# A weight tile's low part is subtracted after the next tile's VectorE steps, and ScalarE adds 1e-9 to the softmax sums

## The chip, the cores and the metric

The kernel runs on one core of a Trainium2 chip (trn2). The metric is the device time of one execution in microseconds (us); lower is better. The engines are TensorE (PE; PEld is its loading of weights), VectorE (DVE), ScalarE (ACT), GpSimd (POOL) and SyncE (SP, which here issues the DMAs).

## The reference

Causal attention by blocks of 64 positions feeds two dense blocks of the kind "linear, nonlinearity, linear". All inputs and outputs are float32.

```python
# q, k, v: (4, 8, 576, 64)
scores = np.where(mask, scale * q @ k.T, -1e9)      # mask: block_i >= block_j
scores = scores - scores.max(-1, keepdims=True)
attn = np.exp(scores)
attn = attn / (attn.sum(-1, keepdims=True) + 1e-09)
x = (attn @ v)                                       # as 2304 tokens x 512
h = np.maximum(x @ w_in, 0.0);  x = (h * h) @ w_out  # w_in 512x2048, w_out 2048x512
h = x @ w_in2                                        # second block, same sizes
g = (a0 + a1*h + a2*h**2 + a3*h**3) / (1 + |b0|*|h| + |b1|*h**2 + 1e-6)
out = g @ w_out2
```

The weights arrive as 64-bit floats (8 bytes for each element, read as pairs of 32-bit words).

## The kernel before

**Products.** A product that must be accurate is made of three reduced-precision products. Each operand is kept as a high part (a rounded copy) and a low part (the original minus that copy), and `PAIRS = ((0, 0), (1, 0), (0, 1))` sums high times high, weight-low times data-high, and weight-high times data-low (L482, L495, L707, L747, L816). The first ten of the 32 heads ("plain", the "float32 heads" of the change) are computed in plain float32 instead, without parts.

**Stages.** A list of slots runs through the attention: in each slot one or two 128-row tiles of one head get their scores (PE, L294), their row maxima (DVE, L315), their exponentials with row sums (ACT, L328), their transposes (PE L370, copied out of PSUM by ACT, L388 and L400) and, some slots later, the product with v (PE, L429 or L442). Between these, the matmuls of the first half of the first dense block (`ha`, `ya`, L482 and L495) are dealt out step by step. After the attention come the second half of that block (`hb`, `yb`, L707 and L747) and then the second dense block (`hc`, `yc`, L707 and L816).

**Normalizing a plain head pair.** After the exponentials of an odd head, DVE adds 1e-9 to the sums of both heads (L340) and takes the reciprocal (L341), POOL spreads these over 64 columns each (`rb`, L344), PE transposes the spread tile (`rows`, L436), ACT copies it (L437), and DVE multiplies the product with v by it (L438, `xp`). POOL then makes the high and low parts of the result (`xt`, L451 and L452). POOL also scales the queries of later heads (`qr`, L228) ahead of the scores.

**Converting a weight tile.** `Converter.step` handles one tile of 128x512 weights per call. ACT makes the magnitude of the upper words (L117), DVE runs four instructions (L118 and L119 on the raw words, L121 and L122 on the result tile `cv`), and SP's queue brings the raw tile (L93). L122, "the bits", is the last: after it `cv` is a float32 tile, and the raw buffer (three of them) is free for a later tile. In the *next* call ACT copies `cv` to the high part (L110) and POOL subtracts to get the low part (L111). The tiles are named `ai` and `ao` (first half of block one, w_in and w_out), `bi` and `bo` (second half), `ci` and `co` (block two).

**Order.** The code is written slot by slot, but a scheduler that simulates the engines decides the order in which each engine's queue holds its instructions; each queue then runs in order. `issue_after` in the code ties an instruction to another for that scheduler.

Of the kernel before, what the change touches and what calls it, by code (L numbers as in the profile page):

```python
# [9 lines left out]
F32R = mybir.dt.float32r  # L10
U32 = mybir.dt.uint32
AF = mybir.ActivationFunctionType
ALU = mybir.AluOpType
# [4 lines left out]
P = 128  # L18
# [7 lines left out]
HALF = NM // 2  # L26
# [18 lines left out]
def f(ap):  # L45
    return ap.bitcast(F32)
# [3 lines left out]
def attention_moe_moe(ctx: ExitStack, tc: tile.TileContext, q, k, v, wi1, wo1, wi2, wo2, a, b, out):  # L50
    nc = tc.nc
# [17 lines left out]
    cab = const.tile([P, 8], F32, name="cab")  # L69
# [6 lines left out]
        name=nc.get_next_instruction_name(), act_func_set_id=EXP_LN_SET, ins=[], outs=[]))  # L76
# [4 lines left out]
    class Converter:  # L81
# [21 lines left out]
                self.step()  # L103

        def step(self):
            if self.mid:
                c, (nm, _, wp, kind, store, key, eng) = self.mid
                self.mid = None
                w = wp.tile([P, 2, 512], F32R, tag="w" + kind, name=f"w_{nm}", bufs=HALF)
                nc.scalar.activation(w[:, 0, :], c, AF.Copy)  # L110
                eng.tensor_tensor(w[:, 1, :], c, f(w[:, 0, :]), op=ALU.subtract)  # L111
                store[kind, key] = w
            if self.raws:
                raw, job = self.raws.pop(0)
                c = self.pool.tile([P, 512], F32, tag="cv", name=f"cv_{job[0]}", bufs=2)
                low, high, cu = raw[:, :, 0], raw[:, :, 1], c.bitcast(U32)
                nc.scalar.activation(c, high.bitcast(F32), AF.Abs, scale=65536.0)  # L117
                nc.vector.tensor_scalar(low, low, 2.0 ** -29, 7.0, op0=ALU.mult, op1=ALU.min)  # L118
                nc.vector.scalar_tensor_tensor(  # L119
                    low, high, 0x80000000, low, op0=ALU.bitwise_and, op1=ALU.bitwise_or)  # L120
                nc.vector.tensor_scalar(c, c, 2.0, 122880.0 * 65536.0, op0=ALU.max, op1=ALU.min)  # L121
                nc.vector.scalar_tensor_tensor(  # L122
                    cu, cu, 3, low, op0=ALU.logical_shift_left, op1=ALU.bitwise_or)
                if job[2] is None:

                    nc.sync.dma_start(job[4][job[5]], c)
                else:
                    self.mid = (c, job)
            self.load()

    PAIRS = ((0, 0), (1, 0), (0, 1))
# [10 lines left out]
    for pool in (attn, early):  # L142
        psets.append([])
        for t in range(5):
            w_ = P * (t + 1)
# [12 lines left out]
    def ptile(un, t):  # L158
        own = psets[un.hd % 2 if un.hd < H else 0]
        if un.gis == (0, 1) and un.hd % 4 > 1:  # L160
            return own[4][:, 0:3 * P] if t == 2 else own[3][:, P * t:P * (2 * t + 1)]
        return own[t]
# [94 lines left out]
    for st in sts:  # L257
        nc.vector.memset(st, 1.0)

    sums = [attn.tile([P, 2, 2, 8], F32, name=f"sums{n}") for n in range(2)]  # L260
    for sm in sums:
        nc.vector.memset(sm, 1.0)
# [70 lines left out]
    def emit_norm(i):  # L333
        st = stats.pop(i)
        un, gi = slots[i]
        if un.plain:
            if un.hd % 2 and gi % 2:
                sm = sums[un.hd // 2 % 2]
                t0, t1 = TILES[gi // 2]
                nc.vector.tensor_scalar(sm[:, 1, :, t0:t1], sm[:, 0, :, t0:t1], 1e-9, None, op0=ALU.add)  # L340
                nc.vector.reciprocal(sm[:, 1, :, t0:t1], sm[:, 1, :, t0:t1])  # L341
                rb = attn.tile([P, t1 - t0, P], F32, tag="rb", name=f"rb{un.hd}_{gi}", bufs=2, padded_shape=[P, 3, P])
                for t in range(t0, t1):
                    nc.gpsimd.tensor_scalar(  # L344
                        rb[:, t - t0].rearrange("p (n d) -> p n d", n=2),
                        sm[:, 1, :, t:t + 1].to_broadcast([P, 2, D]), 1.0, 0.0, op0=ALU.mult, op1=ALU.add)
                spread[un.hd, gi // 2] = rb
            return
        g = GROUPS[slots[i][1]]
        n = len(g)  # L350
        nc.vector.tensor_scalar(st[:, 4:4 + n], st[:, 2:2 + n], 1e-9, None, op0=ALU.add)
        nc.vector.reciprocal(st[:, 6:6 + n], st[:, 4:4 + n])  # L352
        for n, t in enumerate(g):
            r = D if t == 0 else 0
            pv = ptile(slots[i][0], t)[r:P, 0:P * t + D]
            nc.gpsimd.tensor_scalar(pv, pv, st[r:P, 6 + n:7 + n], 0.0, op0=ALU.mult, op1=ALU.add)  # L356
# [221 lines left out]
    for i in range(NI + 5):  # L578
# [7 lines left out]
        if 0 <= i - 1 < NI:  # L586
            emit_norm(i - 1)
# [88 lines left out]
    def tmp(tag, n, nm, dt=F32):  # L676
        return g2.tile([P, n], dt, tag=tag, name=nm, bufs={"t": 3, "o": 1}.get(tag, 2), padded_shape=[P, 512])
# [43 lines left out]
    for u in range(len(units) + LAG):  # L721
        if u < len(units):
            j, m = units[u]
            t0, n = blocks2[j]
# [9 lines left out]
        if u >= LAG:  # L734
            j, m = units[u - LAG]
            t0, n = blocks2[j]
# [33 lines left out]
    mid, gf = {}, {}  # L770
    for u in range(len(units) + LAG):
# [7 lines left out]
        if u - 1 in mid:  # L779
            r, w, t = mid.pop(u - 1)  # L780
# [7 lines left out]
        if u < len(units):  # L788
            j, m = units[u]
            t0, n = blocks3[j]  # L790
# [7 lines left out]
            ab, w, t = tmp("ab", n, f"ab{u}"), tmp("w", n, f"wq{u}"), tmp("t", n, f"t{u}")  # L798
# [7 lines left out]
        if u >= LAG:  # L806
            j, m = units[u - LAG]
            t0, n = blocks3[j]
# [76 lines left out]
```

## Time and profile before

| what | value |
|---|---|
| median of 3 runs | 1020.05 us (1020.04 to 1020.3) |
| the profiled execution's own time | 1022.03 us |
| its span, first to last instruction | 1020.2 us |
| PE busy in the span | 995.7 us (98%) |
| DVE, ACT, POOL busy | 727.6, 722.2, 582.6 us |

The span is the stretch that the trace covers; the remaining 1.8 us of the profiled execution lie around it. "Idle before" in a row is time in which the engine stood still ahead of that instruction, with the releaser that ended it. The ends of matmuls are modelled, so PE can read as busy while its matmuls are not at their densest.

### The profile page before, as it was taken

How to read it: one execution, taken by the hardware profiler on the slowest of the kernel's cores; microseconds unless marked ns; L12 is line 12 of the kernel's file. 1: busy time of each engine (PE TensorE's matmuls, PEld its weight loads, DVE VectorE, ACT ScalarE, POOL GpSimd, SP SyncE). 2: the span in 40 equal slices, each digit the busy share in tenths (PEclk: the TensorE clock that was granted, in tenths of full speed). 3: DMA queues.
4: the chain of work that ended last, by engine and by line, in shares of the span. 5: the costliest groups of instructions: out<-in, count | busy, mean ns of one | idle time of the engine just before them, and what ended most of it. 6: DMA issues, size and time to landing. Idle time of an engine off the chain costs nothing. (4 is left out here: it accounts for less than half of the span.)

```text
span 1020.2 us, 17058 instructions
## 1 busy us (share of the span) xinstructions
PE 995.7 (98%) x5721; PEld 884.1 (87%) x5721; DVE 727.6 (71%) x1412; ACT 722.2 (71%) x1620; POOL 582.6 (57%) x632
## 2 busy tenths in 40 slices
PE   7999999999999999999999999999999999999997
PEld 5677999999999999999788888887888888899996
DVE  6798587768767646786667666887766766777766
ACT  7779687768777746564455557787787776788775
POOL 5677686768676745630232448767466554655552
PEclk9999999999999999999999999999999999999999
DMA  9766334243432204457655572001101100100000
GB/s 302 221 201 210 120 99 150 92 117 111 118 93 81 67 31 149 167 193 247 234 174 187 171 249 95 1 1 41 42 1 32 42 1 1 50 24 1 32 1 31
DMA packets 63894, 106.58 MB, mean 104 GB/s; under 512 B 16064, under 2 KB 34496, under 8 KB 63808
## 3 DMA queue, kind: packets, MB, share of 16 engines
q1 hardware_dynamic: 63520, 105.34, 32.0%
q8 instruction: 45, 0.74, 0.3%
q14 instruction: 41, 0.34, 0.1%
q10 hardware_dynamic: 288, 0.16, 0.1%
HBM read 79.17 MB, written 23.07 MB: 100 GB/s over the span
## 5 line engine op out<-in xcount | busy, mean ns | idle before, releaser
L816 PE MATMUL yc<-w_co,gc 128*128 128x512 f32 x864 | 211.8, 391 | 3.1 <-ACT gc L776 3.1
L707 PE MATMUL hc<-xc,w_ci 128*128 128x512 f32 (+1 forms) x960 | 211.2, 368 | 0.0
L707 PEld LDWEIGHTS hc<-xc,w_ci 128*128 128x128 f32 x960 | 176.1, 188 | 26.3
L816 PEld LDWEIGHTS yc<-w_co,gc 128*128 128x128 f32 x864 | 161.1, 188 | 36.0 <-ACT gc L776 4.6
L777 POOL TENSOR_TENSOR gc<-t,gc 128x512 fp32r<-128x512 f32 (+1 forms) x78 | 105.0, 1353 | 126.1 <-issue 103.3
L482 PE MATMUL ha<-xt,w_ai 128*128 128x320 f32 (+1 forms) x768 | 123.1, 305 | 0.8 <-POOL xt L451 0.6
L495 PE MATMUL ya<-ga,w_ao 128*128 128x320 f32 (+1 forms) x768 | 117.6, 302 | 3.5 <-ACT r L508 1.9
L482 PEld LDWEIGHTS ha<-xt,w_ai 128*128 128x128 f32 x768 | 107.8, 189 | 5.8 <-issue 3.0
L802 POOL TENSOR_TENSOR wq<-wq,ab 128x512 f32<-128x512 f32 (+1 forms) x78 | 96.4, 1235 | 28.7 <-ACT wq L800 28.7
L495 PEld LDWEIGHTS ya<-ga,w_ao 128*128 128x128 f32 x768 | 107.7, 192 | 5.2 <-ACT r L508 2.1
L747 PE MATMUL yb<-gb,w_bo 128*128 128x512 f32 (+1 forms) x480 | 105.9, 368 | 1.1 <-DVE yp L752 1.1
L707 PE MATMUL hb<-xb,w_bi 128*128 128x512 f32 (+1 forms) x480 | 105.5, 367 | 0.0
L747 PEld LDWEIGHTS yb<-gb,w_bo 128*128 128x128 f32 x480 | 87.6, 188 | 13.1 <-ACT gb L509 1.5
L776 ACT ACTIVATE gc<-t 128x512 fp32r<-128x512 f32 (+1 forms) x80 | 47.1, 589 | 72.9 <-DVE t L785 72.9
L803 DVE TENSOR_TENSOR t<-hc,t 128x512 f32<-128x512 f32 (+1 forms) x80 | 50.9, 636 | 66.0 <-ACT t L801 66.0
L707 PEld LDWEIGHTS hb<-xb,w_bi 128*128 128x128 f32 x480 | 87.4, 188 | 11.2
L356 POOL TENSOR_SCALAR p<-p,stat 64x64 f32<-64x64 f32 (+4 forms) x110 | 62.2, 567 | 43.4 <-DVE stat L352 15.8
L370 PE MATMUL tp<-ident,p 128*128 128x128 f32 x480 | 79.2, 281 | 1.1 <-DVE pt_plain L390 0.7
L783 DVE SCALAR_TENSOR_TENSOR wq<-wq,ab 128x512 f32<-128x512 f32 (+1 forms) x80 | 55.2, 691 | 33.8 <-ACT ab L782 21.9
L402 DVE TENSOR_TENSOR pt<-tp,pt 128x384 fp32r<-128x384 f32 (+3 forms) x176 | 58.8, 366 | 20.3 <-ACT pt L400 17.5
L400 ACT ACTIVATE pt<-tp 128x384 fp32r<-128x384 f32 (+3 forms) x176 | 53.8, 346 | 24.4 <-PE tp L370 22.9
L785 DVE SCALAR_TENSOR_TENSOR t<-t,coef,ab 128x512 f32<-128x512 f32 (+1 forms) x80 | 66.8, 835 | 1.7
(137 smaller groups left out, 1983.2 us busy)
## 6 DMA issues: line engine op xcount, KB each, us to landing
kr<-in_k_dram SPq DMA_DIRECT2D x32, 288.0 KB, 3.8
raw_ci<-in_wi_dram SPq DMA_DIRECT2D x16, 512.0 KB, 4.4
raw_co<-in_wo_dram SPq DMA_DIRECT2D x16, 512.0 KB, 3.6
qr<-in_q_dram SPq DMA_DIRECT2D x24, 320.0 KB, 3.3
raw_ai<-in_wi_dram SPq DMA_DIRECT2D x8, 512.0 KB, 4.8
raw_ao<-in_wo_dram SPq DMA_DIRECT2D x8, 512.0 KB, 4.4
raw_bi<-in_wi_dram SPq DMA_DIRECT2D x8, 512.0 KB, 3.5
raw_bo<-in_wo_dram SPq DMA_DIRECT2D x8, 512.0 KB, 3.4
```

The source lines that it names most:

```text
L356: nc.gpsimd.tensor_scalar(pv, pv, st[r:P, 6 + n:7 + n], 0.0, op0=ALU.mult, op1=ALU.add)
L370: nc.tensor.transpose(ps[:, P * n:P * (n + 1)], ptile(slots[i][0], t)[:, P * c:P * (c + 1)], ident)
L402: nc.vector.tensor_tensor(low, src, f(high), op=ALU.subtract)
L482: nc.tensor.matmul(ps[:, 0:n], w[:, zw, P * kk:P * (kk + 1)], xt[:, zx, kk, first:end], start=i == 0, stop=i == 3 * KK - 1)
L495: nc.tensor.matmul(ps[:, 0:n], wA["o", m][:, zw, P * c:P * (c + 1)], gs[m][:, zg, 0:n], start=i == 0, stop=i == 3 * HALF - 1)
L707: nc.tensor.matmul(ps[:, 0:n], w[:, zw, P * kk:P * (kk + 1)], xt[:, zx, kk, 0:n], start=i == 0, stop=i == 3 * KK - 1)
L747: nc.tensor.matmul(acc[j, c][:, 0:n], wB["o", m][:, zw, P * c:P * (c + 1)], g[:, zg, 0:n], start=m == 0 and i == 0, stop=last and i == 2)
L777: (nc.vector if u - 2 >= len(units) - END else nc.gpsimd).tensor_tensor(g[:, 1, 0:n], t, f(g[:, 0, 0:n]), op=ALU.subtract)
L783: nc.vector.scalar_tensor_tensor(w, w, Q0, r, op0=ALU.add, op1=ALU.mult)
L785: nc.vector.scalar_tensor_tensor(t, t, a0, r, op0=ALU.add, op1=ALU.mult)
L802: (nc.vector if u >= len(units) - END else nc.gpsimd).tensor_tensor(w, w, ab, op=ALU.mult)
L816: last = nc.tensor.matmul(acc[j, c], g[:, zg, P * c:P * (c + 1)], w3["o", m][:, zw, :], start=m == 0 and i == 0, stop=m == NM - 1 and i == 2)
```

## The change

It does two things. In `Converter.step`, the part that makes a tile's high and low parts now stands behind the next tile's four DVE instructions, and the subtraction on POOL is given a dependency on the last of them (`bits`): it starts only when the next tile's bits are done. The last tile of a converter has no next tile and no such wait. And for the plain heads, the addition of 1e-9 is an ACT instruction with a bias tile `eps` in place of the DVE instruction; the reciprocal stays on DVE. One memset on DVE fills `eps`.

```diff
         def step(self):
-            if self.mid:
-                c, (nm, _, wp, kind, store, key, eng) = self.mid
-                self.mid = None
-                w = wp.tile([P, 2, 512], F32R, tag="w" + kind, name=f"w_{nm}", bufs=HALF)
-                nc.scalar.activation(w[:, 0, :], c, AF.Copy)
-                eng.tensor_tensor(w[:, 1, :], c, f(w[:, 0, :]), op=ALU.subtract)
-                store[kind, key] = w
+            mid, self.mid, bits = self.mid, None, None
             if self.raws:
...
-                nc.vector.scalar_tensor_tensor(
+                bits = nc.vector.scalar_tensor_tensor(
                     cu, cu, 3, low, op0=ALU.logical_shift_left, op1=ALU.bitwise_or)
...
+            if mid:
+                c, (nm, _, wp, kind, store, key, eng) = mid
+                w = wp.tile([P, 2, 512], F32R, tag="w" + kind, name=f"w_{nm}", bufs=HALF)
+                nc.scalar.activation(w[:, 0, :], c, AF.Copy)
+                rest = eng.tensor_tensor(w[:, 1, :], c, f(w[:, 0, :]), op=ALU.subtract)
+                if bits is not None:
+                    tc.add_manual_dep(rest.ins, bits.ins.name, mybir.DependencyInfo(
+                        mybir.DependencyClass.Sync, mybir.DependencyReason.DATA), reason="behind the next tile's bits")
+                store[kind, key] = w
...
+    eps = cab[:, 4:5]
+    nc.vector.memset(eps, 1e-9)
...
-                nc.vector.tensor_scalar(sm[:, 1, :, t0:t1], sm[:, 0, :, t0:t1], 1e-9, None, op0=ALU.add)
+                nc.scalar.activation(sm[:, 1, :, t0:t1], sm[:, 0, :, t0:t1], AF.Identity, bias=eps)
```

Since the scheduler sees the new dependency and the new engine, it orders the queues anew. Its orders differ from those of before in two stretches: the conversion of `ai` and `ao` (the plain heads and the first product stage behind them) and that of `bi` and `bo` (around the end of the attention); elsewhere only a few neighbours change places. In the changed kernel's rows the lines are numbered anew: L110 is L126, L111 is L127, L117 is L111, L118, L119, L121 and L122 are L112, L113, L115 and L116, L294 is L299, L341 and L344 are L346 and L349, L429 and L436 are L434 and L441, L451 and L452 are L456 and L457, L508 to L510 are L513 to L515. In a row, the number behind a name is the tile's own number, and the one behind the last underscore is a buffer's.

The first place is PE's queue at the second pair of plain heads (heads 2 and 3, their `rows3`). Before:

```order
L370 MATMUL tp7_0_367<-ident_70,p4_2_115 128x128 x3
L429 MATMUL pv3_0_378<-pt_plain_121,vs2_255 64x320
L436 MATMUL rows3_0_385<-ident_70,rb3_1_319 128x128 x3
L294 MATMUL sx14_451<-kr7_310,qr7_309 128x64
L294 MATMUL sx14_451<-kr7_310,qr7_309 128x192
L294 MATMUL sy15_464<-kr7_310,qr7_309 128x320
L429 MATMUL pv3_0_378<-pt_plain_121,vs2_255 64x320
```

In the changed kernel, the same place on PE:

```order
L375 MATMUL tp7_0_368<-ident_70,p4_2_115 128x128 x3
L434 MATMUL pv3_0_379<-pt_plain_121,vs2_256 64x320
L299 MATMUL sx14_452<-kr7_311,qr7_310 128x64
L299 MATMUL sx14_452<-kr7_311,qr7_310 128x192
L299 MATMUL sy15_465<-kr7_311,qr7_310 128x320
L441 MATMUL rows3_0_386<-ident_70,rb3_1_320 128x128 x3
L434 MATMUL pv3_0_379<-pt_plain_121,vs2_256 64x320
```

The three transposes of `rows3` moved behind the scores of the next head (`sx14`, `sy15`). On POOL, which feeds `rows3` by `rb3` and `sx14` by `qr7`, the queue reads at this place, before:

```order
L111 TENSOR_TENSOR w_ai0_270<-cv_ai0_214,w_ai0_270 128x512
L228 TENSOR_SCALAR qr6_251<-qr6_251 128x384
L451 TENSOR_SCALAR xt0_299<-xp1_0_285 128x320
L452 TENSOR_TENSOR xt0_299<-xp1_0_285,xt0_299 128x320
L344 TENSOR_SCALAR rb3_1_319<-sums1_139 128x128 x3
L228 TENSOR_SCALAR qr7_309<-qr7_309 128x384
L111 TENSOR_TENSOR w_ai1_349<-cv_ai1_273,w_ai1_349 128x512
```

and in the changed kernel:

```order
L127 TENSOR_TENSOR w_ai0_277<-cv_ai0_215,w_ai0_277 128x512
L231 TENSOR_SCALAR qr6_252<-qr6_252 128x384
L349 TENSOR_SCALAR rb3_1_320<-sums1_140 128x128 x3
L456 TENSOR_SCALAR xt0_300<-xp1_0_286 128x320
L457 TENSOR_TENSOR xt0_300<-xp1_0_286,xt0_300 128x320
L231 TENSOR_SCALAR qr7_310<-qr7_310 128x384
L231 TENSOR_SCALAR qr8_344<-qr8_344 128x256
```

The spread `rb3` moved ahead of the two instructions on `xt0`, and the subtraction of `w_ai0`, which now waits for the bits of tile `ai1`, stands ahead of the scaled queries `qr6`, `rb3` and `qr7` as it did before.

The second place is ACT's queue where the last but two of the `ha` results are taken out of PSUM (r3_1_5 is the relu of `ha3_1_5`), near the end of the attention. Before:

```order
L510 ACTIVATE s3_1_4_5900<-r3_1_4_5899 128x256
L110 ACTIVATE w_bo3_5911<-cv_bo3_5855 128x512
L117 ACTIVATE cv_bi4_5914<-raw_bi4_5758 128x512
L508 ACTIVATE r3_1_5_5932<-ha3_1_5_5907 128x256
L509 ACTIVATE ga3_1_5_5931<-r3_1_5_5932 128x256
L510 ACTIVATE s3_1_5_5933<-r3_1_5_5932 128x256
L508 ACTIVATE r3_1_6_5954<-ha3_1_6_5938 128x256
```

In the changed kernel:

```order
L515 ACTIVATE s3_1_4_5901<-r3_1_4_5900 128x256
L513 ACTIVATE r3_1_5_5933<-ha3_1_5_5908 128x256
L514 ACTIVATE ga3_1_5_5932<-r3_1_5_5933 128x256
L515 ACTIVATE s3_1_5_5934<-r3_1_5_5933 128x256
L513 ACTIVATE r3_1_6_5955<-ha3_1_6_5939 128x256
L126 ACTIVATE w_bo3_5918<-cv_bo3_5853 128x512
L514 ACTIVATE ga3_1_6_5954<-r3_1_6_5955 128x256
L515 ACTIVATE s3_1_6_5956<-r3_1_6_5955 128x256
L111 ACTIVATE cv_bi4_5912<-raw_bi4_5759 128x512
```

The high part of tile `bo3` and the magnitude of tile `bi4` moved behind the relus r3_1_5 and r3_1_6. On POOL the place reads, in the changed kernel:

```order
L517 TENSOR_TENSOR ga3_1_3_5879<-s3_1_3_5881,ga3_1_3_5879 128x256
L517 TENSOR_TENSOR ga3_1_4_5899<-s3_1_4_5901,ga3_1_4_5899 128x256
L127 TENSOR_TENSOR w_bi3_5859<-cv_bi3_5792,w_bi3_5859 128x512
L517 TENSOR_TENSOR ga3_1_5_5932<-s3_1_5_5934,ga3_1_5_5932 128x256
L517 TENSOR_TENSOR ga3_1_6_5954<-s3_1_6_5956,ga3_1_6_5954 128x256
L517 TENSOR_TENSOR ga3_1_7_5983<-s3_1_7_5985,ga3_1_7_5983 128x256
L127 TENSOR_TENSOR w_bo3_5918<-cv_bo3_5853,w_bo3_5918 128x512
```

Here the subtraction of `w_bi3`, which now waits for the bits of `bo3`, stands between the low parts of `ga3_1_4` and `ga3_1_5`; before, it stood ahead of `ga3_1_3`, and that of `w_bo3` stood in this place.

The third place is DVE's queue around the bits of the first tile (`ai0`). Before:

```order
L340 TENSOR_SCALAR sums0_138<-sums0_138 128x2x3
L315 TENSOR_REDUCE stat4_126<-sy4_222 64x1
L315 TENSOR_REDUCE stat4_126<-sy4_222 128x1
L341 RECIPROCAL sums0_138<-sums0_138 128x2x3
L121 TENSOR_SCALAR cv_ai0_214<-cv_ai0_214 128x512
L315 TENSOR_REDUCE stat5_127<-sy5_241 128x1
L122 SCALAR_TENSOR_TENSOR cv_ai0_214<-cv_ai0_214,raw_ai0_152 128x512
L315 TENSOR_REDUCE stat6_128<-sx6_257 64x1
L315 TENSOR_REDUCE stat6_128<-sx6_257 128x1
L118 TENSOR_SCALAR raw_ai1_158<-raw_ai1_158 128x512
```

In the changed kernel:

```order
L320 TENSOR_REDUCE stat4_126<-sy4_223 64x1
L320 TENSOR_REDUCE stat4_126<-sy4_223 128x1
L115 TENSOR_SCALAR cv_ai0_215<-cv_ai0_215 128x512
L320 TENSOR_REDUCE stat5_127<-sy5_242 128x1
L116 SCALAR_TENSOR_TENSOR cv_ai0_215<-cv_ai0_215,raw_ai0_153 128x512
L346 RECIPROCAL sums0_139<-sums0_139 128x2x3
L320 TENSOR_REDUCE stat6_128<-sx6_258 64x1
L320 TENSOR_REDUCE stat6_128<-sx6_258 128x1
L112 TENSOR_SCALAR raw_ai1_159<-raw_ai1_159 128x512
```

The addition to `sums0` is gone from DVE, and its reciprocal moved behind the bits of `ai0`.

## Rows read from the trace of the kernel before

**Rows 1.** The page, busy time and share of each engine.

```profile
PE 995.7 (98%) x5721; PEld 884.1 (87%) x5721; DVE 727.6 (71%) x1412; ACT 722.2 (71%) x1620; POOL 582.6 (57%) x632
```

**Rows 2.** Windows: PE, PEld, DVE, ACT, POOL busy us, granted clock, DMA share, GB/s.

```profile
0.00:110.00 110.00, 100.09 (x584) 74.51 (x584) 86.62 (x185) 84.65 (x255) 73.58 (x120) 0.98 0.72 225
...
400.00:425.00 25.00, 23.00 (x159) 22.55 (x158) 16.29 (x17) 13.99 (x34) 17.32 (x15) 0.93 0.38 130
```

**Rows 3.** Waits of PE from 0 to 110 us: total, times, longest.

```profile
PE sy L294 <- DMA kr<-in_k_dram: 3.5, 1, 3.5
PE rows L436 <- POOL rb L344: 2.0, 4, 0.9
PE ya L495 <- DVE s L511: 1.5, 1, 1.5
...
```

**Rows 4.** Timeline around 20 us: start, length, instruction, idle before it.

```profile
21.70 1.52 POOL L344 TENSOR_SCALAR rb<-sums 128x128 f32<-128x128 f32 x3
...
22.04 0.33 PE L436 MATMUL rows<-ident,rb 128*128 128x128 f32 x1 [0.88 <-POOL rb L344]
...
24.25 0.95 PE L294 MATMUL sx<-kr,qr 128*128 128x64 f32 x4 [0.65 <-POOL qr L228]
```

**Rows 5.** Windows of 2 us, behind that.

```profile
24.00:26.00 2.00, 1.75 (x6) 1.09 (x6) 0.58 (x2) 1.13 (x3) 2.00 (x4) 0.70 1.04 401
26.00:28.00 2.00, 2.00 (x10) 1.33 (x10) 0.49 (x1) 1.55 (x7) 2.00 (x5) 0.50 0.66 237
```

**Rows 6.** Timeline from 401.5 to 406.5 us.

```profile
401.80 0.74 POOL L512 TENSOR_TENSOR ga<-s,ga 128x256 fp32r<-128x256 f32 x1 [0.29 <-POOL ga L512]
...
402.25 1.96 PE L495 MATMUL ya<-ga,w_ao 128*128 128x256 f32 x15
...
403.92 0.69 DVE L122 SCALAR_TENSOR_TENSOR cv_bo<-cv_bo,raw_bo 128x512 uint32<-128x512 uint32 x1
404.64 0.63 ACT L110 ACTIVATE w_bo<-cv_bo 128x512 fp32r<-128x512 f32 x1 [2.98 <-DVE cv_bo L122]
...
405.73 0.36 ACT L508 ACTIVATE r<-ha 128x256 f32<-128x256 f32 x1
...
406.14 0.39 PE L495 MATMUL ya<-ga,w_ao 128*128 128x256 f32 x1 [1.93 <-ACT r L508]
```

**Rows 7.** Windows of 2 us, behind that.

```profile
406.00:408.00 2.00, 1.79 (x9) 1.59 (x10) 1.59 (x2) 1.94 (x7) 1.64 (x2) 0.77 0.83 311
408.00:410.00 2.00, 2.00 (x11) 2.00 (x10) 1.86 (x3) 2.00 (x6) 2.00 (x3) 0.50 0.61 201
```

**Rows 8.** Single lines, 0 to 110 us: duration ns min/median/max; then busy us, mean ns.

```profile
L111 POOL TENSOR_TENSOR w_ai<-cv_ai,w_ai x8: 1261/1276/1537, 15.7 to 57.5; 128x512 fp32r<-128x512 f32 x8
...
L121 DVE TENSOR_SCALAR cv_ao<-cv_ao x8: 397/950/1144, 57.5 to 100.0; 128x512 f32<-128x512 f32 x8
...
L340 DVE TENSOR_SCALAR sums<-sums 128x6 f32<-128x6 f32 (+1 forms) x10 | 4.7, 465 | 0.0
```

**Rows 9.** Timeline around 98 us, POOL and DVE.

```profile
97.56 1.27 POOL L111 TENSOR_TENSOR w_ao<-cv_ao,w_ao 128x512 fp32r<-128x512 f32 x1
...
97.79 1.58 DVE L119 SCALAR_TENSOR_TENSOR raw_ao<-raw_ao 128x512 uint32<-128x512 uint32 x1
...
99.30 0.48 DVE L511 SCALAR_TENSOR_TENSOR s<-ha,r 128x320 f32<-128x320 f32 x1
```

**Rows 10.** A single ACT line on 128x2: duration ns min/median/max.

```profile
L536 ACT ACTIVATE cab<-coef x1: 238/238/238, 13.1 to 13.1; 128x2 f32<-128x2 f32 x1
```

**Rows 11.** Waits of DVE from 380 to 560 us; then a window of 10 us.

```profile
DVE raw_co L118 <- DMA raw_co<-in_wo_dram: 14.7, 6, 5.1
...
10.00:20.00 10.00, 9.02 (x55) 6.44 (x54) 8.36 (x22) 9.05 (x34) 5.13 (x9) 1.00 1.04 348
```

**Rows 12.** Timeline around 440 us, DVE and PE.

```profile
438.52 0.69 DVE L122 SCALAR_TENSOR_TENSOR cv_bo<-cv_bo,raw_bo 128x512 uint32<-128x512 uint32 x1
...
442.96 2.24 PE L707 MATMUL hb<-xb,w_bi 128*128 128x384 f32 x12
```

## The prediction

> **What bounds the kernel now.** I read the page first: PE is busy for 995.7 us of the span of 1020.2 us, 98%, and no other engine passes 71% [rows 1]. PE's own work is not touched by the change, so all that can be won is PE's idle time, 24.5 us (1020.2 - 995.7), and what its clock loses. Then I read windows, to see where that idle time lies and whether the change comes near it. From 0 to 110 us, where the plain heads run and tiles `ai` and `ao` are converted, PE is idle for 9.9 us (110 - 100.09); from 400 to 425 us, where `bi` and `bo` are converted, for 2.0 us [rows 2]. The other 12.6 us lie where the orders hardly change; I leave them as they are. Third, PE's waits from 0 to 110 us: 3.5 us are the first load and stay; 2.0 us are `rows` waiting for POOL's spread tile `rb`, 1.5 us is `ya` waiting for DVE [rows 3]. That leaves 6.4 us of idle time within reach, 2.9 us of it in small waits. Last, the granted clock in short windows: behind the wait at 20 to 24 us it stood at 0.70 and then 0.50 for two windows of 2 us [rows 5], and behind the wait at 404 us at 0.77 and 0.50 [rows 7]; 0.50 is the level of 1.2 GHz, 1.00 that of 2.4 GHz. The missing shares cost 2 x (0.30 + 0.50) = 1.6 us and 2 x (0.23 + 0.50) = 1.5 us, if PE had work all the time.
>
> **The 1e-9 on ScalarE.** Ten DVE instructions of 4.7 us in all go [rows 8]; they are tiny (4 or 6 columns), and the mean of 465 ns says that some of them were held up. Ten ACT instructions come. The trace does not show this one; the nearest row is an ACT instruction on two columns, 238 ns [rows 10], so 2.4 us. As a lower bound I take nothing (ACT is free at that moment), as an upper one 2.4 us on the path. ACT is busy for 84.65 of the first 110 us, DVE for 86.62 [rows 2], so neither engine is full, and ACT hides it in its 25 us of slack: I take 0. If that slack were gone, it would be 2.4 us. The reciprocal still has one hop between engines before it, from ACT to DVE, as the addition had. The memset for `eps` is one of several at the start, under the 3.5 us of the first load: 0.
>
> **The subtraction behind the next bits.** It moves work in time and adds none: a subtraction takes 1.26 us at its shortest [rows 8]. What it may give is DVE time. DVE's L121 takes 397 ns at its shortest and 950 ns in the median of the eight `ao` tiles [rows 8], and one place shows why: POOL's subtraction ran from 97.56 to 98.83 us, and DVE's L119, begun at 97.79, took 1.58 us, until 99.37 [rows 9]; an instruction of the same kind and size takes 0.69 us elsewhere [rows 6]. So the subtraction cost DVE 0.9 us there, and the relu's second factor (`s`, L511) came behind it at 99.30; that is the DVE result that `ya` waited 1.5 us for. Once the subtraction starts behind the next tile's bits, the four steps of that tile have passed by. What stands on DVE then, in the order of the changed kernel, is often the reciprocal and two maxima out of PSUM, before the next tile's first step.
>
> The Trainium skill, page "SBUF — State Buffer", section "Who interferes with whom", says that DVE and GpSimd share one pair of ports, that it is locked for a whole instruction, and that whichever starts second is blocked fully, for DVE's instructions with two SBUF inputs and those in a two-port mode. By that rule, L119's row agrees: it ended 0.54 us behind POOL's end, about its own length. But by the same rule a subtraction that starts at the bits only meets the next tile's first step in place of the last one's, if that comes within 1.26 us; then the 0.9 and 0.5 us of DVE relief in the sum below would be nothing and the sum 4.2 us; by the rows alone it is 5.6 us. I stay with the rows, because of the maxima in between.
>
> **First stretch.** (a) The 2.0 us of `rows`: around 22 us `rb3` runs on POOL from 21.70 for 1.52 us and PE waits for each third of it [rows 4]. In the new order `rb3` stands ahead of the two `xt` instructions, and PE has the scores `sx14` and `sy15` to do before it asks for `rows3`. These scores need `qr7`, though, and PE already waited 0.65 us for it [rows 4]; it still comes behind `xt`. I take -1.5 us; bounds 0 and -2.0. (b) `ya` at 99.8 us: -0.9 us, the collision; bounds 0 and -1.5. (c) The small waits, 2.9 us: with 4.7 us and some collisions less on DVE, -0.5; bounds 0 and -2.9. (d) The clock behind 24 us costs 1.6 us; with a thinner gap before it, it may stay up. An even chance: -0.8; bounds 0 and -1.6. Sum: -3.7 us.
>
> **Second stretch.** At 404 us PE stands still for 1.93 us: `ya` needs the PSUM bank that the relu at 405.73 frees. That relu sat in ACT's queue behind the high part of `bo3` (L110), which waited 2.98 us for that tile's bits on DVE, from 403.92 to 404.61 [rows 6]. In the new order the relus r3_1_5 and r3_1_6 stand ahead of that L110, and so does not wait for any tile. The stall goes: -1.9 us, and the clock behind it: -1.5 us [rows 7]. Bounds: 0 and -3.4. What is late next? POOL's low part of `ga3_1_5` now stands behind the subtraction of `bi3`, which waits for the bits of `bo3`: 404.61 + 1.26 + 0.74 (a low part, rows 6) = 406.6 us. PE asks for it after 30 matmuls in the new order (15, 2 and 13 of them), at 0.12 us each (15 starts in 1.96 us less the last one's tail) from 402.25, so near 405.9 us. That would be a stall of 0.7 us, unless the bits come earlier for want of collisions. I put this and its like, POOL held behind bits in the first stretch, at +1.5 us; bounds 0 and +4. In the third part of the conversion there is cover: the bits of the last `bo` end at 439.2 us, with the subtraction at 440.5, and PE asks for tile `bi7` not before 442.96 [rows 12].
>
> **Sum.** -3.7 - 3.4 + 1.5 = -5.6 us. The profiled execution took 1022.03 us, 1.83 us more than its span, and would take 1016.4. The median of the three runs is 1.98 us below that execution, 1020.05, so I forecast 1014.4 us.
>
> **Rivals.** *The waits only change their names.* For it: the first stretch has slots whose DVE, ACT and POOL steps hang on each other, its DMAs run at a share of 1.04 of the 16 engines from 10 to 20 us [rows 11], and by the skill's rule above collisions move rather than go. Then the first stretch gives nothing, in the second the 0.7 us stall by `ga3_1_5` grows to 1.3 us and keeps the clock's dip: 0 - 1.9 + 1.3 = -0.6, or 1019.4 us. Against it: the two big waits are read to their ends, and the new order cuts both chains.
>
> *Slower: POOL's queue is held by the new wait.* A subtraction whose next tile is late stands at the head of POOL's queue, and `qr`, `rb`, `xt` and `ga` behind it wait, and PE for those. A tile can be late by its load: DVE waited 14.7 us in six waits for `co` tiles, one of them 5.1 us [rows 11]. There are 16 tiles in the first stretch; it decides from 7.1 / 16 = 0.44 us of new PE wait for each tile on. At 0.65 us each, what PE waited once for `qr`: 16 x 0.65 - 7.1 = +3.3, or 1023.3 us. Against it: POOL is busy for 73.58 us of 110 [rows 2], so it can catch up, and the products with low parts come many slots later.
>
> *Everything goes.* All 6.4 us and both dips: -6.4 - 1.6 - 3.4 = -11.4, or 1008.6 us.
>
> **How the numbers follow.** About 0.2%, 2.0 us, is what a measurement of this kernel can tell from no change. The forecast (2 to 9 us less) gets 0.56, everything 0.08, the names 0.18, slower 0.18. So faster 0.64, same 0.18, slower 0.18. The range reaches from 1009.0 us, which leaves out half of "everything", to 1021.6 us, which takes in the names and leaves out most of "slower". The forecast's own range is 1011 to 1018 us.
>
> **What would show it.** In the changed kernel: no wait of PE for the relu near 404 us and a granted clock of 1.00 behind it; PE's waits for `rb` from 0 to 110 us below 0.7 us; L121's median for the `ao` tiles near 0.4 us rather than 0.95; ten ACT instructions of about 0.24 us. I am wrong if PE's idle time from 0 to 110 us stays near 9.9 us, or if waits of `sx`, `sy` or `ha` for `qr`, `xt` or weight low parts take its place; then the new wait on POOL's queue did it.

## The result, and the profile after

The changed kernel took 1010.57 us in the median of six executions (1009.7 to 1011.8), beside 1020.17 us for the kernel before: a ratio of 0.9895, 95% interval 0.9879 to 0.9911. It is 9.6 us faster. The forecast was 1014.4 us with a range of 1009.0 to 1021.6. The profiled execution took 1011.05 us, with a span of 1009.2 us: 11.0 us less than the span of before.

The page of the changed kernel, busy time of each engine, answers to [rows 1]:

```profile
PE 989.4 (98%) x5721; PEld 881.1 (87%) x5721; DVE 711.7 (71%) x1403; ACT 723.3 (72%) x1630; POOL 580.2 (57%) x632
```

DVE is busy for 15.9 us less, of which the ten additions were 4.7 us [rows 8]; the rest of its work takes 11.2 us less time. PE is busy for 6.3 us less with the same matmuls.

Where the time was won is read at an instruction that both kernels reach through the same wait for `p`, where the plain heads are over (timeline of PE; first before, then after):

```profile
170.74 0.47 PE L294 MATMUL sy<-kk,qh 128*128 128x448 f32 x1 [1.40 <-ACT p L328]
```

```profile
163.62 0.47 PE L299 MATMUL sy<-kk,qh 128*128 128x448 f32 x1 [1.40 <-ACT p L333]
```

Up to there 7.1 us are won, behind it 3.9 us (11.0 - 7.1). The same 857 matmuls on either side (window from the start; PE, PEld, DVE, ACT, POOL busy, granted clock, DMA share, GB/s), first before, then after:

```profile
0.00:144.13 144.13, 134.22 (x857) 107.93 (x857) 109.67 (x259) 110.14 (x333) 95.44 (x152) 0.99 0.64 198
```

```profile
0.00:136.99 136.99, 129.50 (x857) 106.76 (x857) 104.73 (x250) 111.13 (x343) 94.80 (x152) 1.00 0.68 209
```

PE's idle time went from 9.91 to 7.49 us, its busy time from 134.22 to 129.50. PE's waits from 0 to 110 us, after, answer to [rows 3]:

```profile
PE sy L299 <- DMA kr<-in_k_dram: 5.1, 2, 3.5
PE tp L375 <- DVE pt_plain L395: 0.7, 1, 0.7
...
PE sy L299 <- POOL qr L231: 0.2, 1, 0.2
```

The waits of `rows` for `rb` (2.0 us) and of `ya` for DVE (1.5 us) are gone. A wait of 1.6 us for a load of `kr` is new; it is not in every execution, as a second profile of the changed kernel has none (r1, below). From 380 to 520 us only two waits are left, none of them of `ya` for a relu:

```profile
PE hb L712 <- ACT rb L513: 0.5, 1, 0.5
PE yb L752 <- DVE yp L757: 0.3, 1, 0.3
```

The granted clock holds at both times at which it had fallen [rows 5, 7]; the second place lies some 7 us earlier now, and over all of 380 to 425 us the clock is 1.00, where it was 0.96 before:

```profile
24.00:26.00 2.00, 2.00 (x18) 1.49 (x17) 1.47 (x6) 1.96 (x9) 1.94 (x4) 1.00 0.95 301
26.00:28.00 2.00, 2.00 (x14) 1.47 (x12) 1.00 (x3) 2.00 (x9) 1.83 (x5) 1.00 1.18 344
404.00:406.00 2.00, 2.00 (x19) 2.00 (x19) 1.48 (x3) 0.20 (x1) 2.00 (x2) 1.00 0.24 78
406.00:408.00 2.00, 2.00 (x16) 2.00 (x15) 2.00 (x2) 0.90 (x2) 2.00 (x3) 1.00 0.19 66
```

The two lines that the prediction named (duration ns min/median/max, first and last start), the clamp and the new ACT instruction:

```profile
L115 DVE TENSOR_SCALAR cv_ao<-cv_ao x8: 415/532/1414, 56.4 to 96.4; 128x512 f32<-128x512 f32 x8
```

```profile
L345 ACT ACTIVATE sums<-sums,cab x10: 292/314/329, 11.0 to 93.3; 128x6 f32<-128x6 f32 x5, 128x4 f32<-128x4 f32 x5
```

### The profile page after: what moved, and what is told of

Its sections match the earlier page's. It is cut to its first block, busy times and chain, and to the rows that moved or that the text cites. A ratio compares the mean times of both kernels' runs of the same rounds, so it can differ in the third digit from the quotient of the medians.

```text
span 1009.2 us, 17083 instructions
## 1 busy us (share of the span) xinstructions
PE 989.4 (98%) x5721; PEld 881.1 (87%) x5721; DVE 711.7 (71%) x1403; ACT 723.3 (72%) x1630; POOL 580.2 (57%) x632
## 5 line engine op out<-in xcount | busy, mean ns | idle before, releaser
L500 PE MATMUL ya<-ga,w_ao 128*128 128x320 f32 (+1 forms) x768 | 115.1, 298 | 0.0
```

Of the source, the lines that this page charges most:

```text
L500: nc.tensor.matmul(ps[:, 0:n], wA["o", m][:, zw, P * c:P * (c + 1)], gs[m][:, zg, 0:n], start=i == 0, stop=i == 3 * HALF - 1)
```

## The experiments

Three theories were told apart. A: the wait pays on the chip, because POOL's subtraction then stays off VectorE's four steps. B: the order pays, which the scheduler drew anew and might have drawn as well for another reason. C: VectorE was short of the ten additions. Ratios of e1 to e11 and r1 are to the kernel before on the same chip, five rounds each. "Steps" is the busy time of VectorE's four steps over all 64 tiles, summed from the groups of the profile; "start" is where PE begins the instruction shown above.

| kernel | median us | before us | ratio, 95% interval | steps us | start us | span us |
|---|---|---|---|---|---|---|
| before | | | | 189.9 | 170.74 | 1020.2 |
| changed | 1010.57 | 1020.17 | 0.9895, 0.9879 to 0.9911 | 174.9 | 163.62 | 1009.2 |
| e1, 1e-9 alone | 1019.93 | 1021.22 | 0.9981, 0.9967 to 0.9996 | 196.2 | 170.35 | 1018.3 |
| e2, subtraction alone | 1013.15 | 1021.22 | 0.9918, 0.9899 to 0.9938 | 172.7 | 166.04 | 1011.1 |
| e3, no dependency | 1020.63 | 1021.22 | 0.9996, 0.9981 to 1.0012 | 198.7 | 171.36 | 1021.8 |
| e5, wait for the clamp | 1020.84 | 1021.22 | 0.9990, 0.9970 to 1.0009 | 181.7 | 167.76 | 1015.0 |
| e4, order B, no wait | 1021.84 | 1023.09 | 0.9989, 0.9971 to 1.0006 | 194.3 | 167.95 | 1019.4 |
| e7, order B, wait | 1018.35 | 1023.09 | 0.9944, 0.9923 to 0.9964 | 174.3 | 167.52 | 1015.9 |
| e6, order A, no wait | 1020.41 | 1023.09 | 0.9970, 0.9954 to 0.9986 | 191.4 | 167.50 | 1019.2 |
| e8, order A, wait for the clamp | 1018.89 | 1023.09 | 0.9947, 0.9928 to 0.9965 | 187.8 | 168.29 | 1016.8 |
| r1, changed again | 1010.77 | 1021.96 | 0.9891, 0.9870 to 0.9912 | 176.9 | 163.25 | 1009.0 |
| e10, order A, wait in a tiles | 1016.00 | 1021.96 | 0.9942, 0.9920 to 0.9964 | 188.0 | 165.82 | 1014.5 |
| e11, order A, wait in b, c tiles | 1014.06 | 1021.96 | 0.9918, 0.9898 to 0.9938 | 175.1 | 166.31 | 1010.6 |
| e9, subtraction on VectorE | 1013.56 | 1021.96 | 0.9920, 0.9899 to 0.9941 | 162.6 | 165.65 | 1010.1 |

**Each part alone.** e1 is the kernel before with

```diff
-nc.vector.tensor_scalar(sm[:, 1, :, t0:t1], sm[:, 0, :, t0:t1], 1e-9, None, op0=ALU.add)
+nc.scalar.activation(sm[:, 1, :, t0:t1], sm[:, 0, :, t0:t1], AF.Identity, bias=eps)
```

and the memset of `eps`; e2 is the changed kernel with this edit taken back.

> Only the 1e-9 moves to ScalarE; the weight tiles are converted in the order of before, without the wait. Theory A (the gain is the conversion's: the late subtraction leaves VectorE's four steps alone and the relus come ahead of the conversion's copies): about 1019 us, at most 1.5 us below before, and the stall of ya behind the relu near 404 us stays. Theory B (any edit makes the scheduler draw another order, and the gain is the luck of one order): anywhere from 1010 to 1022 us, with other stalls at other places. Theory C (VectorE was short by the ten small additions in the first 110 us): 7 us less from there, about 1013 us.

> Only the conversion's part: parts of the last tile behind the next tile's steps, subtraction behind the bits; the 1e-9 stays on VectorE. Theory A: nearly all of the gain, 1010.5 to 1012 us, VectorE's busy time from 0 to 110 us about as in the changed kernel plus 4. Theory B: anywhere from 1010 to 1022 us. Theory C: only the 3.5 us near 404 us, about 1017 us.

e1 gained 1.9 us (0.0019 x 1021), e2 8.4 us. C falls: nearly all is the conversion's. e1 is a little above what A allowed, and e2 misses the changed kernel by some 2.8 us (0.9918 against 0.9891), so the 1e-9 is worth some 2 to 3 us by the medians, where I had priced it at nothing on the path and at a share of 0.5 us in the small waits. That size is loose: e1's own interval reaches from 0.4 to 3.4 us, and those of e2 and the changed kernel overlap.

**The dependency.** e3 is the changed kernel without these lines, e5 with the dependency tied to the clamp (the instruction ahead of the bits):

```diff
-                if bits is not None:
-                    tc.add_manual_dep(rest.ins, bits.ins.name, ...)
```

```diff
-                nc.vector.tensor_scalar(c, c, 2.0, 122880.0 * 65536.0, op0=ALU.max, op1=ALU.min)
-                bits = nc.vector.scalar_tensor_tensor(
+                bits = nc.vector.tensor_scalar(c, c, 2.0, 122880.0 * 65536.0, op0=ALU.max, op1=ALU.min)
+                nc.vector.scalar_tensor_tensor(
```

> The whole change without the added wait: the parts are written behind the next tile's steps in the program, but the subtraction may start as soon as its copy is there. Theory A says that the wait keeps POOL off VectorE's steps: without it the collisions come back, VectorE is busy for 5 to 10 us more in all and half of the gain goes, about 1015 us. Rival (the place in the program does it, the wait nothing): 1010 to 1011 us. Theory B: anywhere from 1010 to 1022 us.

> As changed, but the subtraction waits for the next tile's clamp (one step earlier) and so starts beside its last step, the bits. If the collision is what costs: the bits take 1.2 to 1.6 us where POOL starts at the clamp's end, against 0.68 to 0.72 in the median of the changed kernel, VectorE is busy for 5 to 10 us more in all, and the time rises by 1 to 3 us, to 1012 to 1014. If collisions cost nothing on PE's path: 1010 to 1011 us, with the bits longer all the same.

Neither gained anything that can be measured. Without the dependency the whole gain goes, not half of it. One step earlier it goes too, although e5's steps are 8 us shorter in sum than those of before. The expectation of e5 held in part: its bits took 1.30 and 1.24 us in the mean in the `ci` and `co` tiles, but 0.91 and 0.75 in `ai` and `ao`. The medians hide a part of what the two gave, by the clock: its mean was 0.999 or more in only 3 and 2 of their 12 executions, with medians of 1018.5 and 1017.7 us; of before's 29 executions beside them it was so in 16, with 1020.6 us. The dependency thus decides, but these two runs mix its two effects: it makes the scheduler draw another order (by the names in the traces, some 250 of PE's 5721 matmuls stand in another place than in the changed kernel, in e3 as in e5), and it makes POOL wait.

**Order and wait apart.** In e4 the dependency is one that the scheduler sees and no engine waits for. The order that this gives is order B; it is that of e5 but for a few instructions of ACT and POOL. In e6 every engine has exactly the order of the changed kernel (order A), and no wait: the added dependency is left out as in e3, and each instruction is tied to the one ahead of it on its own engine, from a list, which puts no wait into the program. The traces of e6, e8, e10, e11 and r1 have the same order of instructions as the changed kernel's on every engine. e7 is order B by such a list with the wait on the bits, e8 order A with the wait on the clamp.

```diff
-    mybir.DependencyClass.Sync, mybir.DependencyReason.DATA), reason="behind the next tile's bits")
+    mybir.DependencyClass.NoSync, mybir.DependencyReason.DATA), reason="behind the next tile's bits")
```

```diff
+def in_order(nc, tc):
...
+        for one, two in zip(names, names[1:]):
+            tc.add_manual_dep(nc.get_inst_by_name(f"I-{two}"), f"I-{one}", mybir.DependencyInfo(
+                mybir.DependencyClass.NoSync, mybir.DependencyReason.DATA), reason="as listed")
...
         attention_moe_moe(tc, *args)
+        in_order(nc, tc)
```

> As changed, but the added dependency is one that only the scheduler sees: no engine waits for it on the chip. The scheduler then draws another order (order B). Theory A (the wait itself pays, it keeps POOL off VectorE's steps): about 1020 us, as without the dependency. Theory B (the order pays): also about 1020 us, since this order is nearly that of the kernel without the dependency. This run is the reference for order B without the wait.

> Each engine's instructions stand exactly in the order of the changed kernel (order A, prescribed as a list), but the wait of the subtraction on the bits is left out. Theory A (the wait pays): most of the gain goes, 1015 to 1020 us, and VectorE's steps take longer. Theory B (the order pays, the wait on the chip is worth nothing): 1009.5 to 1011.5 us.

> Order B prescribed as a list, and in it the subtraction waits on the chip for the bits. Theory A (the wait pays): 1011 to 1014 us. Theory B (the order pays): 1019 to 1022 us, the stalls of order B (rows behind POOL, ya near 404 us) as before.

> Order A prescribed, the subtraction waits for the clamp, one step ahead of the bits, so that it meets the bits on VectorE. Theory A (collisions count): the bits take 1.2 to 1.6 us in many tiles, and the time is 1012 to 1016 us. Theory B (order alone): 1009.5 to 1011.5 us, although the bits are longer.

Neither theory holds alone. Order A without the wait is 0.30% below before (3.1 us), order B with the wait 0.56% (5.7 us), order A with the wait 1.09% (11.1 us, by r1); order B without it can't be told from before. In order A the wait is worth 8.1 us (0.9970 - 0.9891, of 1022 us), in order B 4.6 us. What the steps took follows the wait, not the order: 174.3 and 174.9 us with it, 191.4 and 194.3 without. And e8, where POOL waits but starts beside the bits, is back at 187.8 us of steps and half of the gain. In times, e6, e7 and e8 lie above what their expectations allowed for theory A, with before at 1023.1 us on that chip; as ratios e6 and e8 lie within it, and e7 just outside.

The clock has a part in these ratios. Its mean was 0.999 or more in 7 of 23 executions of before beside e4 to e8, in 2 of 12 of e4, 9 of 12 of e6, 4 of 6 of e7 and all of e8. Among these executions alone the medians are 1020.9 us for before, 1020.3 for e6, 1017.7 for e7 and 1018.9 for e8; beside r1, 1019.8 for before (3 of 11) and 1010.8 for r1 (5 of 5). Order A alone is then worth 0.6 us, order B with the wait 3.3, e8 2.0 and the changed kernel 9.0. By either count most of the gain in order A comes with the wait; the split is rough, since e6 and r1 ran on different chips.

What the wait does in order A is read at the same 857 matmuls as above, in e6 (window from the start, then the largest of its new waits from 0 to 110 us):

```profile
0.00:140.88 140.88, 130.85 (x857) 107.03 (x857) 108.95 (x250) 111.25 (x343) 96.05 (x152) 1.00 0.68 203
```

```profile
PE pv L435 <- ACT pt_plain L394: 1.8, 2, 1.0
```

The waits of `rows` for `rb` and of `ya` for DVE are gone in e6 too, but others stand in their place, and PE is idle for 10.0 us (140.88 - 130.85), beside 9.9 before; 8.6 without a wait of 1.4 us for a load, which comes and goes. With the wait on the bits it is 7.5 us (5.9 without its load wait of 1.6), and 6.9 in r1 (136.62 - 129.71), which has no such load wait.

One place in the same order shows how. e6 first (timeline; start, length, instruction, idle before it):

```profile
54.38 1.72 POOL L131 TENSOR_TENSOR w_ai<-cv_ai,w_ai 128x512 fp32r<-128x512 f32 x1
...
54.90 1.75 DVE L120 SCALAR_TENSOR_TENSOR cv_ai<-cv_ai,raw_ai 128x512 uint32<-128x512 uint32 x1
...
56.69 0.63 ACT L130 ACTIVATE w_ai<-cv_ai 128x512 fp32r<-128x512 f32 x1 [1.54 <-DVE cv_ai L120]
...
57.11 0.74 DVE L321 TENSOR_REDUCE stat<-sx 128x1 f32<-128x576 f32 x1
...
57.22 0.76 ACT L394 ACTIVATE pt_plain<-tp 128x384 f32<-128x384 f32 x3
...
57.75 0.44 PE L435 MATMUL pv<-pt_plain,vs 128*64 128x256 f32 x2 [0.80 <-ACT pt_plain L394]
```

The changed kernel:

```profile
53.12 0.68 DVE L116 SCALAR_TENSOR_TENSOR cv_ai<-cv_ai,raw_ai 128x512 uint32<-128x512 uint32 x1
...
53.84 0.63 ACT L126 ACTIVATE w_ai<-cv_ai 128x512 fp32r<-128x512 f32 x1 [0.49 <-DVE cv_ai L116]
53.95 1.28 POOL L127 TENSOR_TENSOR w_ai<-cv_ai,w_ai 128x512 fp32r<-128x512 f32 x1 [1.30 <-DVE cv_ai L116]
54.26 0.74 DVE L320 TENSOR_REDUCE stat<-sx 128x1 f32<-128x576 f32 x1
...
54.38 0.75 ACT L393 ACTIVATE pt_plain<-tp 128x384 f32<-128x384 f32 x3
```

In e6 the subtraction of the last tile meets the bits of the next: 1.75 us in place of 0.68. ACT's copy stands in its queue and waits 1.54 us for them, the evictions of the plain heads (`pt_plain`) stand behind the copy, and PE waits 0.80 us for one. The chain is POOL, DVE, ACT, PE: what PE waits for is ACT's. In the changed kernel POOL is held for 1.30 us, and the maximum that then runs beside the subtraction on DVE takes 0.74 us, as long as the same one in e6 at 57.11 us, where the subtraction had ended at 56.10. The second place, near 404 us [rows 6], in e6:

```profile
394.22 1.78 DVE L120 SCALAR_TENSOR_TENSOR cv_bi<-cv_bi,raw_bi 128x512 uint32<-128x512 uint32 x1
...
396.06 0.33 SPq L97 DMA_DIRECT2D raw_bo<-in_wo_dram  x1
...
399.07 3.88 PE L501 MATMUL ya<-ga,w_ao 128*128 128x256 f32 x31
...
399.56 0.83 DVE L116 TENSOR_SCALAR raw_bo<-raw_bo 128x512 uint32<-128x512 uint32 x1 [2.40 <-DMA raw_bo<-in_wo_dram]
...
400.07 1.48 POOL L131 TENSOR_TENSOR w_bi<-cv_bi,w_bi 128x512 fp32r<-128x512 f32 x1
...
400.31 1.52 DVE L119 TENSOR_SCALAR cv_bo<-cv_bo 128x512 f32<-128x512 f32 x1
...
402.90 0.68 DVE L120 SCALAR_TENSOR_TENSOR cv_bo<-cv_bo,raw_bo 128x512 uint32<-128x512 uint32 x1
403.61 0.63 ACT L130 ACTIVATE w_bo<-cv_bo 128x512 fp32r<-128x512 f32 x1 [3.02 <-DVE cv_bo L120]
...
404.15 0.40 ACT L515 ACTIVATE ga<-r 128x256 fp32r<-128x256 f32 x1
...
404.60 0.62 PE L501 MATMUL ya<-ga,w_ao 128*128 128x256 f32 x3 [1.65 <-ACT ga L515]
```

and in the changed kernel, in the same order:

```profile
389.45 0.68 DVE L116 SCALAR_TENSOR_TENSOR cv_bi<-cv_bi,raw_bi 128x512 uint32<-128x512 uint32 x1
...
390.19 0.33 SPq L93 DMA_DIRECT2D raw_bo<-in_wo_dram  x1
...
393.71 1.01 DVE L112 TENSOR_SCALAR raw_bo<-raw_bo 128x512 uint32<-128x512 uint32 x1 [2.98 <-DMA raw_bo<-in_wo_dram]
...
394.63 0.42 DVE L115 TENSOR_SCALAR cv_bo<-cv_bo 128x512 f32<-128x512 f32 x1
...
395.05 4.12 PE L500 MATMUL ya<-ga,w_ao 128*128 128x256 f32 x33
395.57 0.68 DVE L116 SCALAR_TENSOR_TENSOR cv_bo<-cv_bo,raw_bo 128x512 uint32<-128x512 uint32 x1
396.28 0.63 ACT L126 ACTIVATE w_bo<-cv_bo 128x512 fp32r<-128x512 f32 x1 [1.37 <-DVE cv_bo L116]
...
396.33 1.30 POOL L127 TENSOR_TENSOR w_bi<-cv_bi,w_bi 128x512 fp32r<-128x512 f32 x1 [1.90 <-DVE cv_bo L116]
...
396.82 0.40 ACT L514 ACTIVATE ga<-r 128x256 fp32r<-128x256 f32 x1
```

The relu does stand ahead of the copy in e6, as the new order says; but the next ACT instruction, the high part of `ga`, stands behind it, and PE waits 1.65 us for that. The order moved the stall by one instruction, and late bits kept it: they end 4.51 us behind the start of `ya` in e6 (403.58 - 399.07), 1.20 us behind it in the changed kernel. Of these 3.3 us, 1.5 are collisions on the tile's own steps, above all the clamp's 1.52 us in place of 0.42. The other 1.8 come through the raw buffer: the load of the tile is issued 0.06 us behind the last tile's bits, which free a buffer, and its first step starts 3.5 us behind that issue in both kernels; in e6 those bits took 1.78 us in place of 0.68 and ended only 3.07 us ahead of `ya`, not 4.92. So a collision on one tile also makes the next one late. Order B shows the other half (e7, with the wait):

```profile
399.25 1.29 POOL L131 TENSOR_TENSOR w_bi<-cv_bi,w_bi 128x512 fp32r<-128x512 f32 x1 [2.26 <-ACT s L519]
...
400.50 1.42 POOL L521 TENSOR_TENSOR ga<-s,ga 128x256 fp32r<-128x256 f32 x2
...
401.28 3.22 PE L504 MATMUL ya<-ga,w_ao 128*128 128x256 f32 x22 [0.82 <-POOL ga L521]
...
405.61 0.62 PE L504 MATMUL ya<-ga,w_ao 128*128 128x256 f32 x3 [1.10 <-POOL ga L521]
```

There the low parts of `ga` stand behind subtractions that wait for the next tile's bits (the first row names ACT's `s`; the bits, begun at 398.42 us, ended just as late, at 399.11), and PE waits for them, 2.3 us in three waits. In the changed kernel such waits are absent.

**Place by place.** r1 is the changed kernel once more. e10 and e11 have order A by the list and the wait in a part of the tiles:

```diff
-                if bits is not None:
+                if bits is not None and nm[0] == "a":
```

(e11 has `!=`.)

> The changed kernel once more, so that it stands beside the next three on one chip: 0.9895 of before, 1010 to 1013 us, whatever theory.

> The order of the changed kernel prescribed; the subtraction waits for the bits in the ai and ao tiles alone, and not in the bi, bo, ci and co tiles. If the wait pays place by place: the start of the stretch behind 110 us is as early as in the changed kernel (7 us before that of before), the stall of ya near 400 us is back, and the time is 4 to 5 us above the changed kernel's, about 1015 us. If the wait pays in the second stretch alone: about 1019 us.

> The order of the changed kernel prescribed; the subtraction waits in the bi, bo, ci and co tiles alone, not in the ai and ao tiles. If the wait pays place by place: the first 110 us are as without the wait (3 us gained in place of 7), no stall near 400 us, and the time is 3 to 4 us above the changed kernel's, about 1014 us; this and the run before it together lose what the prescribed order without any wait lost, 8 us. If it pays in the first stretch alone: about 1019 us.

e10 is 5.2 us above r1, e11 3.3 us, together 8.5 us, where the order without any wait lost 8.1 us. So the wait pays in both stretches, and what it pays adds up. No run has the list together with the whole wait; if the parts add, the 0.4 us between 8.5 and 8.1 is what is left for the list itself, less than these medians can tell. The stall of `ya` near 400 us came back in e10 only as 0.4 us for ACT and 0.3 for POOL. Of the 5.5 us between the spans of e10 and r1, PE is idle for 2.1 us and busy for 3.4 us (992.4 against 989.0, the same matmuls); what made them longer is not shown. The single profiles agree less well (e10 starts behind the plain heads at 165.82 us, not at 163.6): e10, e11 and e6 each waited 1.4 to 1.6 us for a load of `kr` near 7 us, the changed kernel for one at 20 us, r1 for none, so one execution's start is known to some 1.5 us.

**The subtraction on VectorE.** e9 is the changed kernel with

```diff
-                rest = eng.tensor_tensor(w[:, 1, :], c, f(w[:, 0, :]), op=ALU.subtract)
+                nc.vector.tensor_tensor(w[:, 1, :], c, f(w[:, 0, :]), op=ALU.subtract)
```

and no dependency.

> The subtraction of all 48 tiles runs on VectorE, behind the next tile's bits, so that POOL cannot meet VectorE with it. If all that counts is that POOL's subtraction stays off VectorE's steps: 1008 to 1011 us. If VectorE's own time counts as much (48 subtractions of about 0.69 us, what one of its steps with two inputs takes, are 33 us more of VectorE, against some 15 us of collisions saved): 1012 to 1018 us, with waits of PE for VectorE's results from 0 to 110 us.

Its page:

```profile
PE 990.6 (98%) x5721; PEld 882.3 (87%) x5721; DVE 726.4 (72%) x1451; ACT 723.6 (72%) x1630; POOL 518.7 (51%) x584
```

VectorE does 48 subtractions more and ten additions less, and is busy for 1.2 us less than before: the four steps fell from 189.9 to 162.6 us. The time is 8.4 us below before and 2.8 us above r1, with small waits of `ya` and `ha` for DVE (0.6 and 0.4 us). So taking the subtraction off POOL altogether gives three quarters of the gain, and holding it on POOL is better by the medians; the two intervals overlap a little. No version beat the changed kernel.

## Why the prediction was right, and what it mis-sized

The direction and both stretches were right; the sum, -5.6 us, was too small against -9.6 in the medians: 1010.57 us lies just below the forecast's own range of 1011 to 1018 us, and nearer to "everything goes" (1008.6 us, at a chance of 0.08) than to the forecast (at 0.56). Between the two profiles (-11.0 us) the first stretch fell short by 3.4 us, the second by 0.5, and the new waits, +1.5, did not come. By its steps:

- **First stretch, -3.7 us forecast, -7.1 measured.** (a) The waits of `rows` for `rb`: -1.5 forecast, -2.0 measured; in r1 PE then waits 0.95 us for `qr`, behind `xt`, in place of 0.65, so 1.7 there. (b) `ya` at 99.8 us: -0.9 forecast, the whole 1.5 us went; but it went in e6 too, without the wait, so it is not shown that the collision cost it. (c) The small waits, -0.5: from 2.9 us to 2.4 in the changed kernel's profile (7.49 less 3.5 and 1.6 for loads), to 3.4 in r1. So of the 7.1 us, PE's idle time gave 2.4, and its busy time 4.72. Here a premise failed: "PE's own work is not touched by the change", so that only idle time and the clock could be won. Of the 4.72 us 1.6 are the clock's by rows 5; the other 3.1 us stood in no term. They lie in many groups of matmuls that ran a little shorter, and by e6 (130.85 us busy, clock 1.00) 1.8 us of them came with the order and 1.3 with the wait; what shortens them no run here tells. What I also missed is that the order alone does little but move the waits (e6 is idle for 10.0 us, 8.6 without its load wait). I priced the one collision that I had found (0.9 us) and a token for all the others; the runs show 15.0 us less in the four steps over the kernel, and a path, through ACT's queue, by which one can go on to PE, read at two places. That path was in rows 6, and I used it for one place only. The 1e-9, priced at 0, gave some 2 to 3 us as well.
- **(d) and the clock behind 404 us, -0.8 and -1.5.** Both dips are gone, in the profile and in all 11 executions of the changed kernel, whose mean granted clock is 0.999 or 1.0. But they are not in every execution of before either. Beside e1, 16 of its 29 executions stood at 0.999 or above, with a median of 1020.6 us, and 13 below, with 1023.1 us. Against the median of before the clock is then worth 0.6 us (1021.2 - 1020.6) there, but 2.2 us beside e4 to e8 and beside r1 (1023.1 - 1020.9, 1022.0 - 1019.8). My sum counted both dips in full and was then taken from a median that had them in a part of its executions only; the clocks of the six executions of before beside the changed kernel are not on record, so how much of the 9.6 us the clock gave stays open.
- **Second stretch, -3.4 forecast, -3.9 measured** for all behind the plain heads, nearly all of it up to the first `hb`, which starts 11.2 us earlier (406.57 against 417.78 us). The size was right and the reason half right: that the new order by itself takes the relu out of the copy's way, and that "the stall goes", fell with e6. The order needs the wait, which brings the bits earlier, on this tile and through the raw buffer.
- **New waits, +1.5 us forecast, none measured from POOL's hold** (PE waits for `qr` 0.2 us in one profile and 1.9 in r1, against 0.7 before; in r1 these stand ahead of the first subtraction or behind `xt`, and e6 has 1.0 us without any hold). The 0.7 us stall by `ga3_1_5` needed the bits of `bo3` 2.36 us behind the start of `ya` (404.61 - 402.25); they came 1.20 us behind it (396.25 - 395.05), "for want of collisions", as the text left open: 1.0 us of this by the last tile's bits, which ended 4.92 us ahead of `ya` and not 3.90. e7 shows that the fear was sound: in another order the same hold cost 2.3 us there.
- **ACT's ten instructions** took 314 ns in the median, not 240; no wait of PE names them.

Of the rivals, "the waits only change their names" is out: it allowed 0.6 us, the changed kernel is 9.6 us below before and 11.1 as r1, and VectorE's time fell. It does describe much of what the order did without the wait, in e6. The rule that stood behind it, of the Trainium skill, page "SBUF — State Buffer", section "Who interferes with whom", agrees with the traces where two such instructions meet: in e6 the bits begun at 54.90 us, with POOL's subtraction running until 56.10, ended at 56.65, 0.55 us behind it, about their own length. What the rival drew from it, that the collisions would only move, was wrong in the main. The clamp and the bits of all tiles took 16.1 us less than before; the first two steps took 1.1 us more, and the second step of the `ai` tiles 0.95 us in the mean in place of 0.69, so some did move. What VectorE runs beside a held subtraction can be a maximum out of PSUM, as at 54.26 us, which the same page of the Trainium skill says never contends. "POOL's queue is held" is out in this order. "Everything goes" (1008.6 us) was nearest in the first stretch.

The signs that the prediction named came out so: no wait for the relu near 404 us and a clock of 1.00 behind it; no wait for `rb`; the clamp's median for the `ao` tiles at 0.53 us, between 0.4 and the 0.95 of before; PE's idle time down by 2.4 us rather than near 9.9.

## What to carry to other kernels

Where an instruction on GpSimd meets VectorE's, look for what stands behind VectorE's instruction on a third engine's in-order queue: the collision of 1 us was paid there, by an eviction that had nothing to do with either. Look too for the buffer that the late instruction frees: the next load waited for it here. A wait that keeps the two apart can pay more than it costs, but tie it to the last instruction of the burst (one earlier lost half or all of the gain) and let the scheduler know of it, so that it fills the held queue. Before a new order is praised or blamed, prescribe it without the wait, and the wait in another order: here, by the ratios, the order alone gave 3.1 us and the wait in another order 5.7, where both gave 11.1 (0.6, 3.3 and 9.0 at an equal clock).

## What the runs showed of the hardware that was not expected

The time of one kernel spreads with the clock: the 13 executions of before with a mean granted clock below 0.999 were 2.5 us above the other 16. And a load of `kr` near 7 us kept PE waiting for 1.4 to 1.6 us in e6, e10 and e11 (and in e2 and e3), but not in r1, whose loads stand in the same order as those of e6, e10 and e11; the start behind the plain heads moves with it.
